# Finer loads at the head of a kernel: a second x chunk in two loads, a first tile in passes of 384 and 128 tokens, and all of B in 128-row transposing loads

## The chip, the cores and the metric

The kernel runs on one core of one Trainium2 chip. The metric is the device time of one execution in microseconds (us). Every timed run also records the span of the core from its first to its last instruction; the time is the span plus 1.7 to 1.9 us.

## The reference, cut to what matters

The output mixes two branches by a gate. Branch a is a linear state-space layer: with complex diagonal decay it computes `Bu = x @ B^T`, a scan over 2048 tokens, and `y = 2 Re(h @ C^T)`. Branch b is a small mixture layer that changes 8 of the tokens.

```python
dt = jnp.exp(log_dt)
Lam_bar = jnp.exp(dt * Lam)
B_bar = ((Lam_bar - 1.0) / Lam)[:, None] * Bmat
Bu = jnp.einsum("bld,pd->blp", x + 0j, B_bar)
...
    h = Lam_bar[None, :] * h + Bu[:, t, :]
...
y = 2.0 * jnp.einsum("blp,dp->bld", hseq, Cmat).real + x * Dskip[None, None, :]
...
return g * a + (1 - g) * b
```

x is 2048 x 1024; B and C have a real and an imaginary plane of 1024 x 1024 each, all bf16. In the kernel the first product is called S1 and the last S2.

Of the kernel before, what the change touches and what calls it, by code (L numbers as in the profile page):

```python
# [10 lines left out]
F32 = mybir.dt.float32  # L11
# [5 lines left out]
P = 128  # L17
LC = 256
# [6 lines left out]
def kernel(  # L25
# [19 lines left out]
    nc = tc.nc  # L45
# [3 lines left out]
    NCT = NP_ // P  # L49
    KD = D // P  # L50
    NK = L // LC
    NTT = L // P
    BPC = LC // P
# [5 lines left out]
    x2d = A_x[0]  # L59
# [7 lines left out]
    ps_s1 = ctx.enter_context(tc.tile_pool(name="ps_s1", bufs=2, space=PSUM))  # L67
# [3 lines left out]
    X = {}  # L71
    BT = [const.tile([P, KD, NP_], BF16, name=f"BT{pl}", tag=f"BT{pl}") for pl in range(2)]
# [6 lines left out]
    def load_B(pl, c0, c1):  # L79
        nc.sync.dma_start_transpose(BT[pl][:, :, c0 * P:c1 * P], Bsrc[pl][c0 * P:c1 * P, :])  # L80
# [6 lines left out]
    def new_X(m):  # L87
        X[m] = const.tile([P, KD, 2 * LC], BF16, name=f"X{m}", tag=f"XP{m}")

    def load_xT(k):  # L90
        m, kk = divmod(k, 2)
        nc.sync.dma_start_transpose(X[m][:, :, kk * LC:(kk + 1) * LC], x2d[k * LC:(k + 1) * LC, :])  # L92
# [4 lines left out]
        load_xT(2 * m + 1)  # L97

    new_X(0)
    load_xT(1)  # L100
    load_B(1, 0, 1)
    for c0, c1 in ((1, 2), (2, 3), (3, 4), (4, 6), (6, 8)):
        for pl in range(2):
            load_B(pl, c0, c1)
    load_X(1)
# [44 lines left out]
    def warm(n):  # L150
        for _ in range(n):
            nc.tensor.matmul(wps[:], lhsT=wt0[:, 0:P], rhs=wt0[:], start=True, stop=True)
# [110 lines left out]

    vp = {}

    def s1u(m, ct, pl, k0, k1):
        if (m, ct) not in vp:
            vp[m, ct] = ps_s1.tile([P, 2, 2, LC], F32, name="vps", tag="vps")
        o = vp[m, ct][:, pl, k0:k1, :].rearrange("p k t -> p (k t)")
        for dc in range(KD):  # L270
            nc.tensor.matmul(o, lhsT=BT[pl][:, dc, ct * P:(ct + 1) * P], rhs=X[m][:, dc, k0 * LC:k1 * LC], start=(dc == 0), stop=(dc == KD - 1))  # L271

    def s1e(m, ct):
        for kk in range(2):
            k = 2 * m + kk
            if k not in V:
                V[k] = big_new("V", k)
            nc.scalar.copy(out=V[k][:, :, ct, :], in_=vp[m, ct][:, :, kk, :])  # L278
        vp.pop((m, ct))

    def s1(m, ct):
        for pl in range(2):
            s1u(m, ct, pl, 0, 2)
        s1e(m, ct)
# [111 lines left out]

    tab_neg(0)
    warm(1)
    s1u(0, 0, 0, 0, 1)
    warm(2)  # L400
    s1u(0, 0, 0, 1, 2)
    s1u(0, 0, 1, 0, 2)
    s1e(0, 0)
    d0_cp(0, 2)
    tab_bwd_s(0)
# [489 lines left out]
    for n, (m, k) in enumerate(blocks):  # L895
        free_w.extend(fill.get(n, ()))
        if n == 7:
            for pl in range(2):
                t = const.tile([P, 4, 2, D], BF16, name="wdb", tag=f"BT{pl}")
# [48 lines left out]
```

## The kernel before: what the change touches

S1 needs x and B with the contraction dimension on the partitions. Both lie the other way in HBM, so they come in by transposing DMA, all issued from one queue (SP). Only the first 256 tokens of x are loaded plainly and transposed on TensorE. `P` is 128, `LC` is 256, `KD` and `NCT` are 8, `BPC` is 2; a block `X[m]` holds 512 tokens.

```python
def load_B(pl, c0, c1):          # rows c0*128 .. c1*128 of one plane
    nc.sync.dma_start_transpose(BT[pl][:, :, c0 * P:c1 * P], Bsrc[pl][c0 * P:c1 * P, :])

load_B(0, 0, 1)
...
new_X(0)
load_xT(1)                       # tokens 256..511, one load
load_B(1, 0, 1)
for c0, c1 in ((1, 2), (2, 3), (3, 4), (4, 6), (6, 8)):
    for pl in range(2):
        load_B(pl, c0, c1)
load_X(1)                        # block 1, two loads of 256 tokens
for pl in range(2):
    load_C(pl, 0)
```

Further down, in the same queue, come the x of blocks 2 and 3 and the other half of C:

```python
load_X(2)
load_C(0, 512)
load_X(3)
load_C(1, 512)
for b in range(4):
    load_x(b)                    # plain loads
```

A load is said to land when its semaphore, the counter that a consumer waits for, shows that all of it has arrived.

S1 makes one tile of 128 rows of B at a time, in two PSUM buffers (the memory that the matmuls write) that ScalarE empties (`s1e`). A unit `s1u(m, ct, pl, k0, k1)` is 8 matmuls over the chunks k0 to k1 of 256 tokens. The first tile of block 0 is cut so that work starts as soon as something has landed:

```python
def s1u(m, ct, pl, k0, k1):
    ...
    o = vp[m, ct][:, pl, k0:k1, :].rearrange("p k t -> p (k t)")
    for dc in range(KD):
        nc.tensor.matmul(o, lhsT=BT[pl][:, dc, ct * P:(ct + 1) * P], rhs=X[m][:, dc, k0 * LC:k1 * LC], start=(dc == 0), stop=(dc == KD - 1))
...
warm(1)
s1u(0, 0, 0, 0, 1)               # tokens 0..255
warm(2)
s1u(0, 0, 0, 1, 2)               # tokens 256..511
s1u(0, 0, 1, 0, 2)               # imaginary plane, all 512
s1e(0, 0)
```

After the eight tiles of block 0 comes S1 of block 1, and then `gate_rows`, 32 small matmuls that read x of all four blocks.

## Time and profile before

| | kernel before |
|---|---|
| time, median of the 3 runs at hand | 247.49 us (247.4 to 248.19) |
| span of the profiled run | 246.1 us (its time was 247.9 us) |
| TensorE busy | 240.6 us, 98% |
| VectorE busy | 226.2 us, 92% |
| first S1 matmul | 5.93 us |
| tile 1 of S1 begins | 10.62 us |
| wait for B_im of tile 4, by matmul starts | 0.89 us |

The profile's lines are shown in the prediction. How to read the table: with TensorE busy for 98% of the span and the chain of waits running through TensorE from 23.61 us on, everything after that point is one unbroken queue of work. The time then depends on when that queue starts and on every moment in which it stands still.

### The profile page before, as it was taken

What the parts mean: (1) busy time and instruction counts of PE and PEld (TensorE: products, weight loads), DVE (VectorE), ACT (ScalarE), POOL (GpSimd) and SP (SyncE); (2) the same over time, 40 slices, a digit from 0 to 9 for tenths busy, and PEclk for the clock granted to TensorE, in tenths of its full rate; (3) what the DMA queues carried; (4) which work ended last, traced back from release to release, by engine and by line L of the source; (5) the groups of instructions that cost most, each with busy time, mean ns of one, the idle gap of its engine ahead of it and who ended that gap; (6) DMA issues with size and microseconds to landing.
All of it is one profiled execution on the core that took longest, in us unless ns stands there. A gap on an engine that the chain in (4) does not pass through costs nothing.

```text
span 246.1 us, 3533 instructions
## 1 busy us (share of the span) xinstructions
PE 240.6 (98%) x1381; PEld 112.2 (46%) x1381; DVE 226.2 (92%) x230; ACT 119.3 (48%) x206; POOL 26.8 (11%) x47
## 2 busy tenths in 40 slices
PE   8998999999999999999999999999999999999994
PEld 5443444444444444444444444444444444446453
DVE  1799999999999999999999999999999999999932
ACT  3699973333462572223355462235267445456421
POOL 4000000000000301620002040100100211110210
PEclk9999999999999999999999999999999999999999
DMA  7899999999760450666257979778599999962052
GB/s 195 194 149 226 230 244 273 202 239 284 236 181 0 106 153 0 134 125 224 77 188 218 351 226 338 237 224 314 184 390 286 363 306 296 89 142 37 3 133 82
DMA packets 65313, 48.48 MB, mean 197 GB/s; under 512 B 50560, under 2 KB 52224, under 8 KB 65296
## 3 DMA queue, kind: packets, MB, share of 16 engines
q1 hardware_dynamic: 59968, 37.20, 58.1%
q0 software_dynamic: 3264, 7.38, 14.3%
q10 hardware_dynamic: 2064, 3.68, 4.1%
q8 instruction: 11, 0.18, 0.3%
q14 instruction: 6, 0.05, 0.1%
HBM read 27.55 MB, written 8.40 MB: 146 GB/s over the span
## 4 chain that ended last, share of the span: by engine, by line
PE 89%; SPq 7%; DMA 2%; issue 0%; DVE 0%
PE zps L767 42%; PE vps L271 39%; SPq L80 6%; PE zps L783 3%; PE pgu L659 3%; DMA BT<-in_A_B_im_dram 2%; PE y L671 1%; SPq L92 1%; PE zr L485 1%; DVE ot L788 0%; SPq L77 0%; PE xselT_ps L572 0%; PE zs_ps L588 0%; PE zt L492 0%; PE fl_ps L535 0%
## 5 line engine op out<-in xcount | busy, mean ns | idle before, releaser
L271 PE MATMUL vps<-X,BT 128*128 128x512 bf16 (+1 forms) x520 | 112.6, 376 | 1.2 <-DMA BT<-in_A_B_im_dram 0.9
L767 PE MATMUL zps<-CT,H 128*128 128x512 bf16 x480 | 105.0, 379 | 0.0
L271 PEld LDWEIGHTS <-BT 128*128 128x128 bf16 x520 | 50.1, 98 | 61.7 <-DMA BT<-in_A_B_im_dram 1.7
L767 PEld LDWEIGHTS <-H 128*128 128x128 bf16 x480 | 46.5, 98 | 56.6 <-issue 1.3
L278 ACT CAST V<-vps 128x512 bf16<-128x512 f32 x64 | 34.3, 588 | 58.6 <-PE vps L271 58.6
L308 DVE TENSOR_TENSOR_SCAN U<-d,U 128x2048 bf16<-128x2048 f32 (+2 forms) x22 | 62.0, 2860 | 0.6
L772 ACT ACTIVATE ot<-zps,gcol 128x512 bf16<-128x512 f32 x30 | 20.6, 686 | 46.3 <-PE zps L767 46.3
L741 ACT CAST zps<-xd 128x512 f32<-128x512 bf16 (+1 forms) x29 | 16.6, 576 | 3.6 <-ACT xt L728 3.3
L297 DVE TENSOR_TENSOR U<-V,T2tab 128x4096 bf16<-128x4096 bf16 (+2 forms) x11 | 16.6, 1511 | 0.7 <-ACT V L278 0.2
L298 DVE TENSOR_TENSOR V<-V,nTi 128x4096 bf16<-128x4096 bf16 (+2 forms) x11 | 16.7, 1516 | 0.5
L299 DVE TENSOR_TENSOR U<-U,V 128x4096 bf16<-128x4096 bf16 (+2 forms) x11 | 16.7, 1516 | 0.4
L793 POOL DMA_DIRECT2D out_dram<-ot x14 | 12.9, 923 | 32.5 <-ACT ot L772 30.4
L333 DVE TENSOR_TENSOR U<-U,S2tab 128x4096 bf16<-128x4096 bf16 x7 | 16.0, 2292 | 0.2
L335 DVE TENSOR_TENSOR H<-H,U 128x4096 bf16<-128x4096 bf16 x7 | 16.0, 2292 | 0.2
L728 ACT ACTIVATE xt<-xt,omgcol 128x1024 bf16<-128x1024 bf16 x14 | 16.0, 1144 | 0.0
L331 DVE TENSOR_TENSOR H<-U,Ctab 128x4096 bf16<-128x4096 bf16 x7 | 16.0, 2284 | 0.0
L705 POOL DMA_DIRECT2D xt<-in_A_x_dram x12 | 7.1, 594 | 80.9 <-DMA out_dram<-xt 42.9
L366 DVE TENSOR_TENSOR_SCAN U<-D,U 128x1024 bf16<-128x1024 f32 x4 | 8.9, 2279 | 0.1
L723 DVE TENSOR_TENSOR xd<-xt,Dbc 128x1024 bf16<-128x1024 bf16 x14 | 9.0, 683 | 0.0
L659 PE MATMUL pgu<-wgu,xsel 128*32 128x448 bf16 x128 | 7.2, 355 | 0.0
L783 PE MATMUL zps<-CT,H 128*128 128x256 bf16 (+1 forms) x48 | 7.1, 308 | 0.0
L718 POOL DMA_DIRECT2D out_dram<-xt x2 | 1.5, 752 | 49.2 <-DVE xt L717 49.2
(152 smaller groups left out, 127.6 us busy)
## 6 DMA issues: line engine op xcount, KB each, us to landing
wgu<-in_B_w_gate_dram SPq DMA_DIRECT2D x16, 448.0 KB, 3.5
wgu<-in_B_w_up_dram SPq DMA_DIRECT2D x16, 448.0 KB, 6.1
out_dram<-ot POOLq DMA_DIRECT2D x14, 256.0 KB, 6.0
wdb<-in_B_w_down_dram SPq DMA_DIRECT2D x7, 512.0 KB, 10.6
xt<-in_A_x_dram POOLq DMA_DIRECT2D x12, 256.0 KB, 4.3
out_dram<-xt ACTq DMA_DIRECT2D x12, 256.0 KB, 5.2
wd<-in_B_w_down_dram SPq DMA_DIRECT2D x5, 512.0 KB, 7.8
xt<-in_A_x_dram SPq DMA_DIRECT2D x4, 256.0 KB, 4.1
```

The source lines that it names most:

```text
L271: nc.tensor.matmul(o, lhsT=BT[pl][:, dc, ct * P:(ct + 1) * P], rhs=X[m][:, dc, k0 * LC:k1 * LC], start=(dc == 0), stop=(dc == KD - 1))
L278: nc.scalar.copy(out=V[k][:, :, ct, :], in_=vp[m, ct][:, :, kk, :])
L297: nc.vector.tensor_tensor(out=u, in0=v, in1=T2tab[:, :, c0:c1, :], op=ALU.mult)
L298: nc.vector.tensor_tensor(out=v, in0=v, in1=bc(nTi, c0, c1), op=ALU.mult)
L299: nc.vector.tensor_tensor(out=u, in0=u, in1=V[k][:, ::-1, c0:c1, :], op=ALU.add)
L308: nc.vector.tensor_tensor_scan(out=fl, data0=d0[:, c0:c1, :].rearrange("p c t -> p (c t)"), data1=fl, initial=0.0, op0=ALU.mult, op1=ALU.add)
L331: nc.vector.tensor_tensor(out=h, in0=g, in1=bc(Ctab, c0, c1), op=ALU.mult)
L333: nc.vector.tensor_tensor(out=g, in0=g, in1=S2tab[:, :, c0:c1, :], op=ALU.mult)
L335: nc.vector.tensor_tensor(out=h, in0=h, in1=G[k][:, ::-1, c0:c1, :], op=ALU.add)
L741: nc.scalar.copy(out=z[:], in_=xd[b][:, d_:d_ + w])
L767: nc.tensor.matmul(zps[:], lhsT=H[k][:, pl, ct, tl * P:(tl + 1) * P], rhs=CT[pl][:, ct, dsl], start=(fresh and ct == 0 and pl == 0), stop= ...
L772: nc.scalar.activation(out=ots[b][:, dsl], in_=zps[:], func=ACT.Copy, scale=gcol[:, b:b + 1])
```

## The change

Its intent: get rid of the waits at the head. The second x chunk comes in two loads of 128 tokens so that its first half can be used sooner; the first tile is cut to suit (384 tokens, then 128); and all B tiles come alone, so that no tile waits for the rows of its neighbour.

```diff
     new_X(0)
-    load_xT(1)
+
+    def load_x1(tl):
+        nc.sync.dma_start_transpose(X[0][:, :, (BPC + tl) * P:(BPC + tl + 1) * P], x2d[(BPC + tl) * P:(BPC + tl + 1) * P, :])
+
+    load_x1(0)
     load_B(1, 0, 1)
-    for c0, c1 in ((1, 2), (2, 3), (3, 4), (4, 6), (6, 8)):
+    load_x1(1)
+    for c0, c1 in ((c, c + 1) for c in range(1, NCT)):
         for pl in range(2):
             load_B(pl, c0, c1)
...
+    def s1t(ct, pl, t0, t1):
+        ...                       # as s1u, in token blocks of 128
...
     warm(1)
-    s1u(0, 0, 0, 0, 1)
-    warm(2)
-    s1u(0, 0, 0, 1, 2)
-    s1u(0, 0, 1, 0, 2)
+    for pl in range(2):
+        s1t(0, pl, 0, 3)
+    for pl in range(2):
+        s1t(0, pl, 3, 4)
     s1e(0, 0)
```

More of the change, by code (lines that the diff above doesn't have):

```diff
@@ L264 @@
     vp = {}
+    def s1t(ct, pl, t0, t1):
+        if (0, ct) not in vp:
+            vp[0, ct] = ps_s1.tile([P, 2, 2, LC], F32, name="vps", tag="vps")
+        o = vp[0, ct][:, pl].rearrange("p k t -> p (k t)")[:, t0 * P:t1 * P]
+        for dc in range(KD):
+            nc.tensor.matmul(o, lhsT=BT[pl][:, dc, ct * P:(ct + 1) * P], rhs=X[0][:, dc, t0 * P:t1 * P], start=(dc == 0), stop=(dc == KD - 1))
     def s1u(m, ct, pl, k0, k1):
```

## The prediction

> **What bounds the kernel now.** I read the page first, for the busy shares and the chain of waits, then TensorE's timeline over the first 45 us, the issuing queue's timeline beside it, the waits of that stretch, and engine sums over short windows.
>
> ```profile
> PE 240.6 (98%) x1381; PEld 112.2 (46%) x1381; DVE 226.2 (92%) x230; ACT 119.3 (48%) x206; POOL 26.8 (11%) x47
> ...
> q8 instruction: 11, 0.18, 0.3%
> ...
> PE 89%; SPq 7%; DMA 2%; issue 0%; DVE 0%
> ```
>
> TensorE is busy 98% of the span, and the chain that ended last is TensorE work for 89% of it. The other 9% (SPq and DMA) is the run-up: the chain comes out of the queue that issues the loads and enters TensorE at 23.61 us with the B tile that it waited for longest. From there the chain in order of time has no wait until the last evictions at 243 us. So the only time that this change can reach is TensorE's lost time before 23.61 us. TensorE's timeline shows it:
>
> ```profile
> 5.93 1.05 PE L271 MATMUL vps<-X,BT 128*128 128x256 bf16 x8
> 6.82 0.38 PE L152 MATMUL wps<-wt 128*128 128x256 bf16 x2
> 7.44 1.03 PE L271 MATMUL vps<-X,BT 128*128 128x256 bf16 x8 [0.24 <-DMA X<-in_A_x_dram]
> 8.65 1.90 PE L271 MATMUL vps<-X,BT 128*128 128x512 bf16 x8 [0.18 <-DMA BT<-in_A_B_im_dram]
> 10.48 0.20 PE L436 MATMUL vb_ps<-ident,vrow 8*128 8x8 bf16 x2
> 10.62 12.26 PE L271 MATMUL vps<-X,BT 128*128 128x512 bf16 x56
> 23.61 21.76 PE L271 MATMUL vps<-X,BT 128*128 128x512 bf16 x100 [0.73 <-DMA BT<-in_A_B_im_dram]
> ```
>
> The first S1 tile (ct 0) takes from 5.93 to 10.48 us in three pieces, each begun by a landing: B_re, the second x chunk (7.44), B_im (8.65). The next 56 matmuls follow each other without a hole, 216 ns from start to start in the trace, to the first half of tile 4. Then TensorE stands still for B_im of tiles 4 and 5. The marked 0.73 us counts from a modelled end. By starts, the 56th matmul began at 22.50, the next could have begun at 22.71 and began at 23.61: **0.89 us** lost. In the first tile, 16 matmuls of 512 tokens are 3.46 us, against 4.55 taken.
>
> ```profile
> 2.57 2.60 SPq L92 DMA_TRANSPOSE X<-in_A_x_dram  x1
> 5.21 1.31 SPq L80 DMA_TRANSPOSE BT<-in_A_B_im_dram  x1
> ...
> 13.33 1.31 SPq L80 DMA_TRANSPOSE BT<-in_A_B_im_dram  x1
> 14.68 3.56 SPq L80 DMA_TRANSPOSE BT<-in_A_B_re_dram  x1
> 18.29 2.42 SPq L80 DMA_TRANSPOSE BT<-in_A_B_im_dram  x1
> 20.75 2.18 SPq L80 DMA_TRANSPOSE BT<-in_A_B_re_dram  x1
> ```
>
> The issuing queue is solid. A 128-row load costs it 1.31 us (1.35 to the next), a 256-row load 2.18 to 3.56. B_im of tile 4 is issued only at 18.29, behind the whole pair 4-5 of B_re, and its semaphore comes at 23.56.
>
> ```profile
> 16.90:17.10 0.20, 0.20 (x2) 0.08 (x1) 0.20 (x1) 0.20 (x2) 0.00 (x0) 1.00 7.34 47
> 17.10:18.30 1.20, 1.20 (x7) 0.58 (x6) 1.17 (x4) 1.17 (x3) 0.00 (x0) 1.00 0.31 13
> ...
> 22.60:23.40 0.80, 0.28 (x2) 0.00 (x0) 0.80 (x3) 0.80 (x3) 0.00 (x0) 1.00 1.37 65
> ```
>
> The last two columns are DMA share and GB/s. Twice the loads nearly stop, at 17.0-18.4 and 22.6-23.4 us, each after an instruction packet (16 KB at 16.72, 8 KB at 22.09 in the trace). The second hole is what held B_im of tile 4 until 23.56.
>
> **What the Trainium skill says.** "DMA: Bandwidth & Descriptors", Anatomy of one DMA: the semaphore fires only once the last byte has landed. The trace agrees: the x chunk, issued at 2.57, releases its matmul at 7.44, 4.8 us later[...]. "Perfetto Trace Analysis", What "DMA-bound" means: a solid sequencer track is descriptor generation, not data movement. The trace agrees here too: bursts reach 290 GB/s, while 256 KB per 1.35 us is 194. "TensorE: Matmul & The Clock Gate", Back-to-back issue gap: N/2.4 + 2.5 ns warm for one matmul, but about 81 ns sustained for N=128 with weight loads. Here the trace decides for the first: 216 ns at 512, 109 at 256, and 56 at 128 (the 16 x transposes at 4.11, which load weights each time). "Runtime: NRT & Kernel Launch", Instruction fetch mechanics: engines refill instructions in 16 KiB blocks of 256. Eleven q8 packets of 16 KB fit TensorE's 2762 instructions (10.8 blocks), so I take the 16.72 packet for TensorE's.
>
> **The change, part by part.**
>
> (1) x loads. One 2.60 us issue becomes two of 1.31, with B_im of tile 0 between. Issues: x 1a 2.57-3.88, B_im 3.92-5.23, x 1b 5.28-6.59; then tile 1's B_re starts at 6.63 instead of 6.57. Landings by data order: B_re of tile 0 landed at 5.89 and both halves of x at 7.40 in the trace, so half as much should land about 6.5 (6.2 to 6.8). B_im then has x's old second place, about 7.4. x 1b has B_im's old place, 8.6, plus 0.07: 8.7.
>
> (2) First tile. N=384 is 384/512 x 216 = 162 ns by the scaling above, N=128 is 56. Work: 16 x 0.162 + 16 x 0.056 = 2.59 + 0.90 = 3.49 us, practically the old 3.46. It starts later (6.5, not 5.93: with x 1a in the pass, tokens 0-255 no longer start alone) but runs without inner waits: pass pl 0 6.5-7.8, pl 1 7.8-9.1 (B_im there at 7.4), the 128-token passes 9.1-10.0 (x 1b there at 8.7). Then 0.14 for the two small transposes: 10.15. Tile 1 needs its B_re, landed 10.18 before, now about 10.24. So tile 1 starts at about 10.3 instead of 10.62: **gain about 0.3 us**, and no more than 0.38, because that landing bounds it.
>
> (3) B loads. Four 256-row loads become eight 128-row ones. Issue: 8 x 1.35 = 10.8 us, against 10.74 before (14.68 to 25.42), so the queue is finished at about 25.5 as now. The order changes: B_im of tile 4 is issued at 16.1-17.4 instead of 18.3-20.7. Even behind the 1.4 us hole and two queued loads (0.9 us each at 290 GB/s) it lands about 20.5. TensorE wants it at 10.3 + 12.1 = 22.4. **Gain 0.89 us.** Tiles 5 to 7 come in the same rhythm, 2.7 us per tile against 3.46 us of matmuls, so the slack grows.
>
> Sum: 0.89 + 0.3 = 1.2 us. From it I take 0.2 for point (b) below: about 1.0.
>
> **Does the gain reach the end?** From 23.6 on all TensorE work moves forward together. What might hold it: VectorE, 92% busy and itself hardly waiting for TensorE, won't move earlier. H of each chunk against its S2: chunk 1 is ready at 75.3 and used at 79.4; chunk 6 at 207.0 and 211.8; the last tile's first half at 232.2 and used at 235.8. The smallest slack is 3.6 us, over three times the gain. ScalarE's evictions of tiles 0 and 1 end at 13.5 and 17.06 behind its own table work; the PSUM buffers are wanted again at 13.8 and 17.2. That is 0.1 to 0.3 us of slack, a possible small loss.
>
> **Rivals.** (a) The 128-row loads slow the queue: fewer rows per issue, so x 1 of the next block and C come later. The rows of 2.18 and 2.42 us, under 2 x 1.35, speak for it; the 3.56 that the hole lengthened against it. X of block 1 landed at 32.86; it would be wanted at 34.6 instead of 35.7. If a hole adds its whole 1 us to the issue again, 33.9: still enough. It would cost at most some tenths: 246.7. (b) The instruction packet moves. The first tile has 32 matmuls instead of 24 and one warm matmul instead of three, net 6 matmuls and 6 weight loads more, so the fetch comes about 1.3 us earlier plus the 0.3 gained, near 15.1. Then the 1.4 us hole falls on tile 3's B_re, which landed at 16.13 and is wanted at 17.2: up to 0.4 us of new wait, 246.8. (c) The 128-token passes cost the skill's 81 ns rather than 56: 16 x 25 ns = 0.4 us, eating the whole gain of (2): 246.7. The 16 transposes speak against it. (d) x 1a lands no earlier than about 7.2, because the two halves share the engines with B_re: first tile a loss of 0.3 us, 247.0. (e) All else moves and an engine behind takes over, nothing gained: 247.5. The slacks above speak against it.
>
> **Range and chances.** 247.49 - 1.0 gives 246.5. With everything right and no hole in the way 1.3 us are gained, 246.2; with two of the rivals at once 247.2. The three runs of before spread from 247.4 to 248.19, so I add 0.3 below and 0.2 above. 2% is 4.9 us; all the lost time before 23.61 us is 2 us, so faster by over 2% is impossible by this reading, and slower would need a new wait of 6 us.
>
> **What would show it.** The 0.73 wait for B_im gone and the run of 512-token matmuls unbroken from about 10.3; that run's matmul number 57 at about 22.4 instead of 23.61; the first tile starting at 6.2 to 6.8 in one piece, its 128-token matmuls 56 ns apart; B issues of 1.31 us ending near 25.5; later work earlier by the same 1.0 to 1.2 us to the end. I would be wrong if TensorE waits anew for a B or X tile before 36 us, for a PSUM buffer at tiles 2 or 3, or if a late S2 waits for H.

## The result, and the profile after

The changed kernel took a median of 247.93 us (247.54 to 248.56, 6 runs); the kernel before, in the same rounds and with its earlier runs, 247.49 us (247.4 to 248.7, 6 runs). The ratio is 1.001, with a 95% interval of 0.9986 to 1.0034. Ratios are computed as the mean time of one kernel's runs over that of the other's of the same rounds, so they are not quite the ratios of the medians quoted. Executions over 1.5% slower than the fastest of the same kernel are left out of the means. The predicted 246.5 (245.9 to 247.4) was too low: no gain came.

The profiled run of the changed kernel took 247.54 us, its fastest; its span is 245.8 us. The page's busy shares and its chain by engine:

```profile
PE 238.5 (97%) x1363; PEld 112.7 (46%) x1387; DVE 225.9 (92%) x230; ACT 119.2 (48%) x206; POOL 26.8 (11%) x47
...
PE 95%; DMA 2%; issue 1%; SPq 1%; DVE 0%
```

The queue's share of the chain has shrunk from 7% to 1%, and TensorE's has grown from 89% to 95%: the chain now enters TensorE at 7.25 us, with x, instead of at 23.61 with B. (This trace lacks some matmul records: 1363 matmuls against 1387 weight loads. Where one matters, the weight loads are used.) TensorE's timeline of the changed kernel:

```profile
5.75 0.28 PE L157 MATMUL wps<-wt 128*128 128x256 bf16 x1
7.25 3.65 PE L276 MATMUL vps<-X,BT 128*128 128x384 bf16 x32 [1.22 <-DMA X<-in_A_x_dram]
10.84 0.20 PE L448 MATMUL vb_ps<-ident,vrow 8*128 8x8 bf16 x2
11.20 48.29 PE L283 MATMUL vps<-X,BT 128*128 128x512 bf16 x219 [0.16 <-issue]
59.42 0.83 PE L497 MATMUL zr<-X,rg 128*32 128x512 bf16 x12
```

Two things are as intended. The first tile runs without an inner hole (32 matmuls from 7.25), and there is no wait for B up to 59 us. One thing is not: the first tile starts only at 7.25 us, after 1.22 us of idling for the first half of x. The matmul at 11.20 is the second of tile 1, as the weight loads show:

```profile
10.97 0.98 PEld L283 LDWEIGHTS <-BT 128*128 128x128 bf16 x6
```

So tile 1 starts at 10.98 us, against 10.62 before. It was predicted at 10.3. The queue:

```profile
2.57 1.54 SPq L102 DMA_TRANSPOSE X<-in_A_x_dram  x1
4.15 1.31 SPq L80 DMA_TRANSPOSE BT<-in_A_B_im_dram  x1
5.51 1.31 SPq L102 DMA_TRANSPOSE X<-in_A_x_dram  x1
6.86 1.31 SPq L80 DMA_TRANSPOSE BT<-in_A_B_re_dram  x1
...
16.32 1.90 SPq L80 DMA_TRANSPOSE BT<-in_A_B_im_dram  x1
...
25.62 1.31 SPq L80 DMA_TRANSPOSE BT<-in_A_B_im_dram  x1
26.98 4.36 SPq L92 DMA_TRANSPOSE X<-in_A_x_dram  x2
```

B_im of tile 4 is issued at 16.32 and landed at 20.4 us; TensorE wants it at 23.1. That wait is gone, and in none of the eight traces with 128-row loads for this tile does it come back. But the first half of x, issued at 2.57, landed at 7.12, when the whole chunk had landed at 7.40 before; and the issue of the last B load ends at 26.93 instead of 25.39, so in these two traces everything behind it in the queue is 1.5 us later.

**A sum that holds in every trace.** Taking the starts of TensorE's first matmul of tile 1 and of its very last matmul, the difference is 231.1 us plus the waits in between, in all traces. From the last matmul's start it is 2.4 us to the landing of the last store, then a tail to the end of the span:

span = start of tile 1 + waits after it + 231.1 + 2.4 + tail

| trace | tile 1 starts | waits within S1 of block 0 | wait for x of block 3 | last matmul starts | tail | span |
|---|---|---|---|---|---|---|
| before | 10.62 | 0.89 | 0 | 242.64 | 1.11 | 246.14 |
| before_again | 10.63 | 2.02 | 0 | 243.79 | 1.11 | 247.29 |
| before_third | 11.58 | 0.64 | 0 | 243.35 | 1.11 | 246.85 |
| after | 10.98 | 0 | 0 | 242.10 | 1.29 | 245.77 |
| after_again | 11.16 | 0 | 0 | 242.27 | 1.29 | 245.94 |
| after_third | 11.02 | 0.38 | 1.04 | 243.56 | 1.29 | 247.23 |

The rows "again" and "third" are from the experiments below. The wait is the start of the waiting matmul against the start that an unbroken run of 216 ns per matmul would give it. The table is the whole explanation in small: the change trades a wait that varies from 0.6 to 2 us in these traces for a tile 1 that is later than its usual 10.6, a longer tail, and in one run two new waits. All three traced runs of before (247.90, 249.14 and 248.62 us) were slower than its median, so they lose more at the head than a typical run does; in tail_only below, which has the head of before, B_im is not waited for at all.

### The profile page after: what moved, and what is told of

Read it like the earlier page. It is cut to its first block, busy times and chain, and to the rows that moved or that the text cites. A ratio compares the mean times of both kernels' runs of the same rounds, so it can differ in the third digit from the quotient of the medians.

```text
span 245.8 us, 3528 instructions
## 1 busy us (share of the span) xinstructions
PE 238.5 (97%) x1363; PEld 112.7 (46%) x1387; DVE 225.9 (92%) x230; ACT 119.2 (48%) x206; POOL 26.8 (11%) x47
## 4 chain that ended last, share of the span: by engine, by line
PE 95%; DMA 2%; issue 1%; SPq 1%; DVE 0%
PE vps L283 43%; PE zps L779 42%; PE zps L795 3%; PE pgu L671 3%; DMA X<-in_A_x_dram 2%; PE vps L276 1%; PE y L683 1%; PE zr L497 1%; SPq L80 1%; DVE ot L800 0%; SPq L77 0%; PE xselT_ps L584 0%; PE zs_ps L600 0%; PE zt L504 0%; PE vb_ps L448 0%
## 5 line engine op out<-in xcount | busy, mean ns | idle before, releaser
L283 PE MATMUL vps<-X,BT 128*128 128x512 bf16 x484 | 107.3, 379 | 0.8 <-issue 0.3
L283 PEld LDWEIGHTS <-BT 128*128 128x128 bf16 x496 | 48.0, 98 | 58.7 <-issue 0.8
L753 ACT CAST zps<-xd 128x512 f32<-128x512 bf16 (+1 forms) x29 | 16.6, 576 | 3.6 <-ACT xt L740 3.3
L309 DVE TENSOR_TENSOR U<-V,T2tab 128x4096 bf16<-128x4096 bf16 (+2 forms) x11 | 16.6, 1509 | 0.5
```

The costliest lines, as they stand in the source:

```text
L309: nc.vector.tensor_tensor(out=u, in0=v, in1=T2tab[:, :, c0:c1, :], op=ALU.mult)
L753: nc.scalar.copy(out=z[:], in_=xd[b][:, d_:d_ + w])
```

## The experiments

All outputs are right. There were twelve runs of ten kernels; each group of four shared a chip and the runs of the kernel before.

### The two kernels again

No edit. 

> The kernel before, unchanged: sets the noise of the comparison, and gives a second trace of it. Theory A (the wait for B_im of tile 4 is a fixed 0.9 us in every run): ratio 1.000 within 0.002, the trace again shows about 0.7 us of gap before the 57th S1 matmul and tile 1 starting near 10.6 us. Theory B (the first trace was a slow sample: it took 247.9 us against a median of 247.49, so the wait is often shorter): the gap is under 0.5 us in this trace, or its span is about 245.7 us.

Measured: 247.48 us median (247.02 to 249.14, 7 runs) against 247.69 for the other runs of the same kernel, ratio 0.9993 (0.9974 to 1.0012). The trace was of a run of 249.14 us. TensorE there:

```profile
10.63 12.94 PE L271 MATMUL vps<-X,BT 128*128 128x512 bf16 x55
24.75 35.57 PE L271 MATMUL vps<-X,BT 128*128 128x512 bf16 x161 [1.19 <-DMA BT<-in_A_B_im_dram]
```

An unbroken run would have reached the 57th matmul at 10.63 + 56 x 0.216 = 22.73; it began at 24.75, 2.02 us late. Of these 1.35 are the wait for B_im of tile 4 itself, and 0.67 smaller waits before it. Neither theory was right as stated: the gap is not fixed at 0.9, and in this trace it was longer, not shorter. What varies is the landing of that load: 23.56 us in the first trace, 24.71 here. The fastest run of this kernel, 247.02 us, is what the sum gives with no wait at all: 10.62 + 231.1 + 2.4 + 1.11 = 245.2, and 1.77 more is 247.0.

> The changed kernel, unchanged: a second trace and more runs. If x 1a's late landing (7.12 us in the first trace, behind a hole of half a microsecond in the DMA traffic at 6.1 to 6.6 us) is systematic, the first tile again starts at 7.1 to 7.3 us and tile 1 at about 11.0. If the hole was chance, the first tile starts at 6.4 to 6.8 us and tile 1 at about 10.3 to 10.5, and the time is 0.5 us shorter in that run. Ratio to before 1.000 to 1.003 under the first, 0.998 to 1.000 under the second.

Measured: 247.80 us median (247.61 to 248.98, 6 runs), ratio 1.0014 (0.9992 to 1.0035). The first tile started at 7.43 us, tile 1 at 11.16. The late landing of the first half of x came again (7.29 us). It is common and not fixed: the same loads landed it at 7.16 and 7.05 in two further traces, and at 6.36 and 6.56 in x_only and early_x0.

### B alone

```diff
-    for c0, c1 in ((1, 2), (2, 3), (3, 4), (4, 6), (6, 8)):
+    for c0, c1 in ((c, c + 1) for c in range(1, NCT)):
```

(on the kernel before). 

> The kernel before with only the B loads changed to 128 rows each; x loads and the first tile as before. Theory A (parts add up): the wait before tile 4 disappears, tile 1 starts at about 10.6 us as before, the gain is 0.4 (typical run) to 0.9 us (as in the trace): ratio 0.9965 to 0.9985. Rival (the 128-row loads push the next block's x later and cost there): TensorE waits for X of block 1 near 35 us, ratio 1.000 or more.

Measured: 247.51 us median (247.28 to 248.25, 6 runs), ratio 0.9999 (0.998 to 1.0019). In its trace tile 1 starts at 10.58, B_im of tile 4 lands at 19.96 and is not waited for, and the last matmul starts at 241.82, the earliest of all traces and 0.82 before that of the first trace of before. So the B part does in the trace what was predicted of it:

```profile
10.58 48.63 PE L271 MATMUL vps<-X,BT 128*128 128x512 bf16 x220
```

Yet the median is only 0.18 below that of before in the same rounds, and the ratio did not move. One reason can be read off this trace: its tail is 1.36 us instead of 1.11, which the number of DMAs fixes (see "The tail"). A second is argued from the sum: a typical run of before has less to lose than the traced ones. A third is only possible: x of block 3 landed at 58.63, half a microsecond before it was wanted, and may be late in other runs. The rival as stated (x of block 1) did not happen: there is no wait near 35 us.

### x and the first tile alone

```diff
-    for c0, c1 in ((c, c + 1) for c in range(1, NCT)):
+    for c0, c1 in ((1, 2), (2, 3), (3, 4), (4, 6), (6, 8)):
```

(on the changed kernel). 

> The changed kernel with the B loads put back to 256 rows for tiles 4 to 7; x in two loads, the first tile in passes of 384 and 128. Theory A: tile 1 starts at about 11.0 us instead of 10.6, 0.35 us later; the wait for B_im of tile 4 absorbs it (the load's landing does not depend on TensorE), so it shrinks to about 0.4 us and the time stays as before: ratio 0.999 to 1.001. Rival (the late first tile is paid in full): 0.35 us slower, ratio 1.0015 or more.

Measured: 247.62 us median (247.28 to 248.79, 6 runs), ratio 1.0012 (0.9989 to 1.0035). TensorE:

```profile
6.54 2.85 PE L276 MATMUL vps<-X,BT 128*128 128x384 bf16 x16
9.63 1.05 PE L276 MATMUL vps<-X,BT 128*128 128x128 bf16 x16 [0.23 <-DMA X<-in_A_x_dram]
...
11.18 48.29 PE L283 MATMUL vps<-X,BT 128*128 128x512 bf16 x219 [0.36 <-DMA BT<-in_A_B_re_dram]
```

Tile 1 starts at 10.96 (the view lacks its first matmul; the weight load shows it), as in the changed kernel, although here the first half of x landed at 6.36 and the first matmul ran at 6.54: the second half then came at 9.59 (0.40 us of wait by matmul starts) and tile 1's B_re at 10.91 (0.20). In the kernel before that B_re had landed at 10.18. Splitting the x load thus delays what is behind it in the queue: one load of 256 tokens cost the queue 2.40 to 2.64 us in seven traces of eight (3.33 in the other), the two halves together 2.78 to 2.98 in six traces, and 0.04 more for the second issue. Theory A's absorption holds in this trace: B_im of tile 4, still in a 256-row load, landed at 22.91, just before the later TensorE wanted it. The interval of the ratio does not exclude the rival.

### The changed loads with the old start

```diff
-    for pl in range(2):
-        s1t(0, pl, 0, 3)
+    s1t(0, 0, 0, 2)
+    warm(2)
+    s1t(0, 0, 2, 3)
+    s1t(0, 1, 0, 3)
     for pl in range(2):
         s1t(0, pl, 3, 4)
```

(on the changed kernel). 

> The changed kernel, but the first tile begins with tokens 0 to 255 alone (as before), then takes token blocks 2 and 3 as they land. Theory A (the changed first tile is late because its first pass waits for x 1a, which lands at 7.1 to 7.3 instead of 6.5): the first tile starts at 5.9 to 6.7 us again, and tile 1 starts when its B_re has landed, at 10.4 to 10.9 us, 0.1 to 0.5 earlier than in the changed kernel's traces (10.98, 11.16). It stays later than the 10.6 of before, because the split x load costs the queue 0.3 us. Rival (the order of the passes is not what costs; the landing of tile 1's B_re is): tile 1 starts where it did, 11.0 to 11.2.

Measured: 247.88 us median (247.58 to 248.45, 6 runs), ratio 1.0007 (0.9973 to 1.0041). The first matmul is back at 5.97 us and tile 1 starts at 10.78, 0.2 to 0.4 earlier than in the changed kernel: of its later start, that part belongs to the first pass waiting for x, the rest to the split load, as far as one trace can say. But the time did not follow, because this trace has a wait that none before had. The waits of its TensorE after 60 us:

```profile
PE zr L499 <- DMA X<-in_A_x_dram: 0.3, 1, 0.3
```

`gate_rows` reads x of all blocks; its fourth matmul, the first on block 3, began at 60.14 where 59.42 was possible, because x of block 3 landed at 60.09. (The view counts 0.3 from the modelled end of the matmul before; by starts it is 0.72.) A smaller wait, 0.17 us, is for B_im of tile 2: it landed at 16.09, behind the 16 KB instruction packet, which came at 13.82 here instead of at 15.8 to 16.8 as in all other traces. In the kernel before that load had landed at 55.46, and TensorE came to it at 59.98.

### The changed passes with the old loads

```diff
-    s1u(0, 0, 0, 0, 1)
-    warm(2)
-    s1u(0, 0, 0, 1, 2)
-    s1u(0, 0, 1, 0, 2)
+    for pl in range(2):
+        s1t(0, pl, 0, 3)
+    for pl in range(2):
+        s1t(0, pl, 3, 4)
```

(on the kernel before, with `s1t` as in the change). 

> The kernel before with only the passes of the first tile changed to 384 and 128 tokens; x in one load, B as before. Theory A: the first pass waits for the whole x load (7.4 to 7.6 us), the work is 3.6 us, tile 1 starts at 11.0 to 11.2 us, 0.45 later than before; the wait for B_im of tile 4 shrinks by the same 0.45 where there is one, so the time is within 0.5 us of before. Rival (passes are harmless, the split load is what delays): tile 1 at 10.7 or earlier.

Measured: 249.35 us median (247.81 to 250.03, 4 runs), ratio 1.0053 (1.0002 to 1.0105). TensorE:

```profile
7.40 3.65 PE L271 MATMUL vps<-X,BT 128*128 128x384 bf16 x32 [0.77 <-DVE ang L184]
11.12 10.53 PE L278 MATMUL vps<-X,BT 128*128 128x512 bf16 x48
21.98 1.90 PE L278 MATMUL vps<-X,BT 128*128 128x512 bf16 x8 [0.33 <-DMA BT<-in_A_B_re_dram]
25.02 35.35 PE L278 MATMUL vps<-X,BT 128*128 128x512 bf16 x163 [1.14 <-DMA BT<-in_A_B_im_dram]
```

The start is as expected, 7.40 and 11.12. (The view names VectorE's `ang` as what ended the idle time, but these matmuls read only x and B; of what they read, x landed last, at 7.26.) What was not expected is the last two lines: B_re and B_im of tile 4 were late (B_im landed at 24.97), so that the later tile 1 was followed by 1.79 us of waits for B by matmul starts, the most in any trace, and absorbed nothing. In this kernel, as in the kernel before, the load's landing is a matter of luck. Over the six traces with 256-row loads for tiles 4 and 5 it came at 22.6, 22.9, 23.6, 24.3, 24.7 and 25.0 us; over the eight with 128-row loads at 20.0 to 21.8. The queue shows where most of the spread arises. In those six traces the 16 KB instruction packet comes while B_re of tiles 4 and 5 is being issued, and that issue took 3.10 to 4.88 us; B_im was issued behind it, at 17.9 to 19.4, and landed 4.7 to 5.6 us later. The two longest issues (4.61 in before_again and 4.88 here) are those where the packet itself took 2.4 us, against 0.9 to 1.2 in the other four. What delays both no run shows. Two of the four runs also had a granted clock of 0.991 and 0.993, so part of the 0.5% may not be from the head.

### The tail

```diff
-        (nc.sync if b < 4 else nc.gpsimd).dma_start(xt[:], x2d[b * P:(b + 1) * P, :])
+        if b < 3:
+            for c0 in range(0, D, 512):
+                nc.sync.dma_start(xt[:, c0:c0 + 512], x2d[b * P:(b + 1) * P, c0:c0 + 512])
+        else:
+            (nc.sync if b < 4 else nc.gpsimd).dma_start(xt[:], x2d[b * P:(b + 1) * P, :])
```

(on the kernel before). 

> The kernel before with three of its later plain x loads (at 57 us, idle time of the queue) split in two: three more DMAs and nothing else. Theory T (the queue's last waits go through the DMA semaphores in a fixed order, 0.06 us each; the number of DMAs decides how many are still to come after the last store's): the last store is on the last semaphore of the list, landing of the last store to the end of the span 0.92 to 0.94 us instead of 1.11. Rival (the 1.30 and 1.36 us of the changed kernel and of B alone come from something else at the end): 1.11 us as before.

Measured: the tail is 0.93 us, as expected. The time was 247.27 us median (247.14 to 247.89, 4 runs), ratio 0.9988 (0.9944 to 1.0032), which is too coarse for 0.2 us; the tail in the trace is the measurement. At the end of the program the queue waits for the DMA semaphores one after the other, about 0.062 us each, in a fixed order; eight of them are used in turn by the loads and stores of SP and ScalarE. In the kernel before three of these waits are still to come after the last store's, with five more DMAs in the changed kernel six, with four more (B alone) seven, with three more none, with one more (x alone) two. The tails 1.11, 1.29, 1.36, 0.93 and 1.05 us are 0.93 plus 0.06 for each. This trace also shows a wait that the prediction had marked as possible. ScalarE's eviction of tile 0:

```profile
13.32 1.05 ACT L278 CAST V<-vps 128x512 bf16<-128x512 f32 x2
```

It ends at 14.37, and TensorE's first matmul of tile 2, which needs that PSUM buffer and could have begun at 14.16, began at 14.43. Together with 0.11 at tile 3 it cost 0.38 us. B_im of tile 4 landed at 22.64 in this run and was not waited for.

### Only tiles 4 and 5 in 128 rows, and the tail

```diff
-    for c0, c1 in ((1, 2), (2, 3), (3, 4), (4, 6), (6, 8)):
+    for c0, c1 in ((1, 2), (2, 3), (3, 4), (4, 5), (5, 6), (6, 8)):
```

(on the kernel before, with the plain load of b = 0 split as above, so that three DMAs are added). 

> The kernel before with only tiles 4 and 5 of B in 128-row loads, 6 and 7 in 256 rows, and one later plain x load split so that three DMAs are added. Expected by the sum: tile 1 at 10.6 us as before, no wait for B_im of tile 4 (0.89 and 1.35 us in two traces of before), last landing to end 0.93 us: last matmul start 231.1 us after tile 1, at 241.7 to 241.8; span 245.1 to 245.3, time 246.9 to 247.1 in the runs without other disturbance, ratio 0.997 to 0.999. Rival (the B wait is rare in the unprofiled runs, and B on its own gained nothing): ratio 0.999 to 1.001.

Measured: 247.21 us median (246.81 to 248.05, 6 runs) against 247.53 for the kernel before in the same rounds, ratio 0.9981 (0.9946 to 1.0016). The trace:

```profile
10.74 48.77 PE L271 MATMUL vps<-X,BT 128*128 128x512 bf16 x224
```

Tile 1 at 10.74, all 224 matmuls up to `gate_rows` in one piece with no wait for B and 0.26 us for PSUM buffers at tiles 2 and 3; tail 0.93. The last matmul starts at 242.11.

### x of block 3 earlier

```diff
     load_X(2)
-    load_C(0, 512)
     load_X(3)
+    load_C(0, 512)
     load_C(1, 512)
```

On the changed kernel: 

> The changed kernel with the x loads of block 3 moved ahead of the third C load. Theory L (the 128-row loads end the queue's B work 1.0 to 1.8 us later, x of block 3 lands at 56.9 to 60.1 us instead of 55.5, and TensorE wants it at 59.4: in the changed kernel's longer runs it waits there): block 3 lands by 55 us, the runs over 248.3 us become rarer, median 247.5 to 247.7, ratio 0.999 to 1.001. Rival (the longer runs come from elsewhere, or from the first 25 us): same spread and median as the changed kernel, 247.8 to 247.9. Tile 1 at 11.0 to 11.2 and tail 1.29 us in both cases.

Measured: 247.49 us median (247.34 to 249.55, 6 runs), ratio 1.0004 (0.9969 to 1.0038). Block 3 landed at 55.21 in the trace. Four of the six runs lie from 247.34 to 247.59, one at 247.91; the sixth, 249.55, had a granted clock of 0.990. The median is as theory L has it and 0.3 to 0.4 below the changed kernel's, but those were other rounds, and the mean is drawn up by the last run.

On the version with tiles 4 and 5: 

> The version with tiles 4 and 5 of B in 128 rows and three DMAs more, with x of block 3 moved ahead of the third C load too. Expected: tile 1 at 10.6 to 10.75, no wait for B_im of tile 4, none for x of block 3, tail 0.93 us: last matmul start 231.1 us after tile 1 plus 0.1 to 0.3 for PSUM buffers at tiles 2 and 3; median 246.9 to 247.2, ratio 0.997 to 0.999. Rival: no gain over the version without the move (247.2, 0.998).

Measured: 247.34 us median (246.92 to 247.67, 6 runs) against 247.61, ratio 0.9981 (0.9957 to 1.0004). The trace has tile 1 at 10.54, 0.38 us of waits for PSUM buffers, block 3 landing at 52.77, tail 0.93. No difference to the version without the move can be seen.

### A third look at both

> The kernel before once more, for a third trace: B_im of tile 4 landing anywhere from 22.6 to 25.0 us and the wait for it in front of the 57th S1 matmul equal to that landing minus 22.7 (0 if earlier); span equal to tile 1's start plus that wait plus any PSUM wait plus 231.1 plus 3.5.

Measured: one run, 248.62 us. B_im of tile 4 landed at 24.27 and TensorE went on at 24.32. Here even tile 1 was late (11.58), because the whole x chunk landed only at 8.47. The rule as expected (landing minus 22.7) therefore fails; landing minus the time at which TensorE got there, 23.68, holds, 0.64 us. The sum gives 11.58 + 0.64 + 231.1 + 2.4 + 1.11 = 246.8, the span.

> The changed kernel once more, for a third trace: first tile start at 7.1 to 7.4 us, tile 1 at 10.9 to 11.2, no wait for B; tail 1.29 us; the one thing open is whether x of block 3, which landed at 57.9 and 56.9 in the two traces so far, comes after 59.4 us in a long run.

Measured: one run, 249.09 us, the longest of the changed kernel. TensorE:

```profile
7.30 3.65 PE L276 MATMUL vps<-X,BT 128*128 128x384 bf16 x32 [0.43 <-DMA X<-in_A_x_dram]
...
18.31 41.61 PE L283 MATMUL vps<-X,BT 128*128 128x512 bf16 x188 [0.21 <-DMA BT<-in_A_B_re_dram]
...
60.91 1.46 PE L497 MATMUL zr<-X,rg 128*32 128x512 bf16 x21 [0.66 <-DMA X<-in_A_x_dram]
```

This is the changed kernel's long run taken apart. B_re of tile 3 landed at 18.26 and was wanted at 17.93; just before, from 16.6 to 18.0 us, behind a 16 KB instruction packet at 15.84, the loads had moved 5 GB/s. Then x of block 3 landed at 60.87 and held `gate_rows` for 1.04 us. "No wait for B" was wrong, and the open question is answered: x of block 3 does come too late in a long run. With 11.02 + 0.38 + 1.04 + 231.1 + 2.4 + 1.29 the span of 247.2 is accounted for.

## Why the prediction was wrong, point by point

In short: the landings behind the split x load were put too early, so that a gain at tile 1 became a loss; the gain at tile 4 was taken from a typical run that does not have all of it; and the tail and the loads pushed back were not counted.

**Part (1), the landings in the x loads.** This step failed, and it is the largest. "Half as much should land about 6.5 (6.2 to 6.8)" stood for 7.12, 7.29 and 7.16 us in three traces of the changed kernel (7.05, 6.56 and 6.36 in three variants). In the three traces half the bytes bought 0.1 to 0.3 us against the 7.40 and 7.39 of the first two traces of before, not 0.9. In the first trace of the changed kernel the DMA traffic falls just then:

```profile
6.10:6.65 0.55, 0.00 (x0) 0.00 (x0) 0.00 (x0) 0.55 (x2) 0.30 (x1) 1.00 1.11 51
```

That is 51 GB/s, where bursts reach 290. In after_again there is such a hole from 6.2 to 6.9 (30 GB/s), in after_third there are two earlier ones (48 GB/s from 4.7 to 5.1, 97 from 5.5 to 5.8). In x_only and early_x0, where the landing was in the predicted range, it came only behind the landing (66 GB/s from 6.7 to 7.1; 56 from 6.8 to 7.2). So the estimate fits a load with no hole in its way; what makes the hole no run shows. (The section that the prediction cites for a landing is written of DMAs that GpSimd issues; for these loads, issued by SP, the traces alone speak.)

The same part also put the split at 0.06 us of queue time; it cost about 0.46 (2.90 plus 0.04 against 2.48, medians). Tile 1's B_re, put at 10.24, therefore landed at 10.42, 10.83 and 10.38 in the three traces and at 10.43 to 10.91 in the variants. In x_only the first half of x was in time, and tile 1 still began at 10.96, right behind that B_re: an early first half alone would not have brought the gain.

**Part (2), the first tile.** The work was right to the digit: 162 ns and 56 ns between matmul starts, 3.49 us in all, in one piece. But it hangs from the start. Tile 1 came at 10.98, 11.16 and 11.02 instead of 10.3: a loss of about 0.4 us against the usual 10.6, where a gain of 0.3 was put down. This is rival (d), which the prediction named and gave too little weight. Either half of the change is enough to lose the gain: with the old loads and the new passes tile 1 is at 11.12, because the first pass waits for x; with the new loads and the old start it is at 10.78, no earlier than before.

**Part (3), B.** The mechanism was right: the wait for B_im of tile 4 is gone in all three traces and in B alone. The size was off in two ways. First, the 0.89 us were read from a trace whose run took 247.9 us, and were then taken from a median of 247.49, made of other runs. The wait is no constant. It follows the landing of one load, which varied by over 2 us, and the sum puts a run without any wait at 247.0. Half a microsecond separates that from the median of the kernel before, so a typical run cannot have had more than that to gain (this is argued from the sum, since runs without a trace show no waits). Second, "the queue is finished at about 25.5 as now" came out as 26.93, 26.38 and 27.43. The 25.39 of before was itself an early case: in two more traces it was 26.42 and 26.71. By the means of three traces each, about 0.7 us of delay is the change's.

**Does the gain reach the end?** The slacks of VectorE held. But the step listed only consumers that the change moves forward, and checked only x of block 1 among the loads that it pushes back. x of block 3 was wanted at 59.4 instead of 60.0 and landed 2.1 us later (58.6 against 56.4, means of the three traces each), and in one of the three it was too late by 1.04 us.

**What was not in the prediction at all.** The tail: 0.18 us more, in all traces of the changed kernel, from five more DMAs.

**Rivals.** (b): the instruction packet was not at 15.1 as estimated. It came at 16.74, 16.80 and 15.84 us in the changed kernel, against 16.72, 16.10 and 16.84 before. Yet the reading that it goes with TensorE's position fits: in all fourteen traces it began after 90 to 98 of TensorE's weight loads, also in early_x0, whose first tile has 40 matmuls and where it came at 13.82. The size was wrong. The hole behind it did hit tile 3's B_re in one trace, with the 0.4 us named, and tile 2's B_im in early_x0. (c) did not happen. (a) happened to block 3, not to block 1.

The terms together, as an estimate for a typical run: at most -0.5 for B, +0.4 for tile 1, +0.2 for the tail, and new waits in some runs. That fits the +0.1 to +0.4 between the medians; the runs are too noisy to measure each term in the time itself. The range would have needed a typical run as its anchor and rival (d) as a likely case.

**A version that beats both?** Tiles 4 and 5 alone in 128 rows, with the tail put right, had medians 0.3 us below the kernel before in two sets of rounds (ratio 0.9981 both times). Both intervals reach past 1, so it is the best seen, not shown to be faster.

## What to carry to other kernels

When a kernel is one unbroken queue of work on one engine, its time is the start of that queue plus its waits; read those two from several traces before pricing a change, because a wait for a DMA seen once is one draw from a spread, and subtract it from the time of the run in which it was seen. Splitting a load helps only the consumer that waits for its first part, and only if the first part really lands earlier; it makes everything behind it in the issuing queue later, so go down the queue to the last load that has a deadline. Split just the load that is waited for (here tile 4), and leave the others large.

## What the Trainium skill lacked or had wrong

- "TensorE: Matmul & The Clock Gate", Back-to-back issue gap: its sustained spacings with weight loads, about 81 ns for N=128 and 131 for N=512, are not met here. The S1 matmuls of 128 tokens, each with its own weight load, started 56 ns apart, those of 512 tokens 216.
- "Runtime: NRT & Kernel Launch", Instruction fetch mechanics: it calls the cost of crossing a block mostly hidden. Behind the 16 KB packet the transposing loads in flight nearly stopped, for 1.4 us in the first trace of before (47 and 13 GB/s in the two windows that the prediction shows); in after_third a like stop (5 GB/s from 16.6 to 18.0) came before a wait of 0.38 us for B_re of tile 3. That the packet is the cause was not tested.
- No page has what a transposing load of this size costs its issuing queue on this chip: 1.31 us for 128 rows of 1024 bf16, 1.8 to 2.6 us for 256 rows when nothing stalls.
- No page has the tail: about 0.062 us per DMA semaphore still to be waited for, 0.93 to 1.36 us from the last landing to the end of the span, by the number of DMAs over eight semaphores.
